# A static schedule for 32-head attention plus a gated feed-forward: free head order for ScalarE, units that change engine, a third score bank given by rules, and VectorE and GpSimd copies kept apart

## The chip, the cores and the metric

The kernel runs on one core of one Trainium2 chip. The metric is the device time of one execution in microseconds (us). Engines are named as in the profile: PE is TensorE, PEld its weight loads, ACT is ScalarE, DVE is VectorE, POOL is GpSimd, SP is SyncE.

## The reference, cut to what matters

```python
# x: 1 x 2048 x 512, 32 heads of 16; all bf16
g = sigmoid((x * gate_w).sum(-1, keepdims=True))
qkv = x @ wqkv
p = softmax(q @ k.T * 16 ** -0.5)          # 32 heads x 2048 x 2048 scores
a = (p @ v) @ wo
b = ((x @ w_gate) * (x @ w_up)) @ w_down   # inner width 1376
return g * a + (1 - g) * b
```

Attention has 134 million scores, and every one needs an exponential. That work sets the size of this kernel.

Of the kernel before, what the change touches and what calls it, by code (L numbers as in the profile page):

```python
# [10 lines left out]
ALU = mybir.AluOpType  # L11
# [160 lines left out]
FL = []  # L172

# [16 lines left out]
def _build(nc, A_x, A_wqkv, A_wo, W_gate, W_up, W_down, gate_w, out):  # L190
# [14 lines left out]
    NCELL = 46  # L205
    RA = 22
# [12 lines left out]
    with ExitStack() as stack:  # L219
# [18 lines left out]
        PT = sb("PT", [128, NCELL, 512], BF16)  # L238
# [4 lines left out]
        bsb = sb("bsb", [128, 2, 4, D], BF16)  # L243
# [66 lines left out]
        d_wv[0] = load("act", wv[:, :, 0:128], wcol(2 * D, 2 * D + 128), "dwv0", 0.5, 4.0)  # L310
# [18 lines left out]
        r_ = load("act", wv[:, :, 128:D], wcol(2 * D + 128, 3 * D), "dwv1", 0.55, 9.5)  # L329
        d_wv[1:] = [r_] * (NB - 1)  # L330
# [51 lines left out]
        cells = [_Cell() for _ in range(NCELL)]  # L382

        def cell_ap(c, n, dt=None):
            a = PT[:, c : c + n, :].rearrange("p a b -> p (a b)")
            return a if dt is None else a.bitcast(dt)
# [4 lines left out]

        def alloc(n, t, pair=False, keep=0):
            if pair:
                got = None
                for i in range(RA, NCELL, 2):
                    if is_free(i, t) and is_free(i + 1, t):
                        if got is None:
                            got = i
                        if keep == 0:
                            return got  # L400
                        keep -= 1
                return None
            for k in range(RA):
                i = (st["ring"] + k) % RA
                if i + n <= RA and all(is_free(x, t) for x in range(i, i + n)):
                    st["ring"] = i + n
                    return i
                if k > 3:
                    break
            return None  # L410
# [12 lines left out]
        pe = {"mode": "c"}  # L423

# [21 lines left out]
        class Fill:  # L446

            def __init__(self, name, packs, deps, evac, pos):
                self.name = name
                self.packs = packs  # L450
                self.deps = deps
                self.evac = evac
                self.pos = pos
                self.i = 0
                self.bank = None
                self.old = []
# [82 lines left out]
        def f_v(b, tg, pos):  # L539
            packs = []  # L540
            for t4 in range(4):
                t = 4 * tg + t4

                def mk(bk, t=t, t4=t4):
                    def fn(e):
                        r = None
                        for kt in range(KD):
                            for q in range(4):
                                r = e.matmul(
                                    bk.ap[32 * q : 32 * q + 32, t4 * 128 : (t4 + 1) * 128],  # L550
                                    xT[:, kt, t * 128 + 32 * q : t * 128 + 32 * q + 32],
                                    wv[:, kt, b * 128 : (b + 1) * 128],
# [9 lines left out]
                packs.append((mk, 0.36, "c"))  # L562

            def evac(bk, last):
                bk.need += 1
                ev_v[b, tg] = add(
# [3 lines left out]
                        VS[:, 4 * tg : 4 * tg + 4, 8 * b : 8 * b + 8, 0:Dh],  # L570
                        bk.ap.rearrange("p (t h d) -> p t h d", t=4, d=Dh),
# [5 lines left out]
                base = VS[:, 4 * tg, 8 * b, :]  # L577
                src = bass.AP(base.tensor, base.offset, [list(base.ap[0]), [(H + 2) * VW, 4], [1, 2 * VW]])
                for k in range(3):
                    dst = VD[:, k, 4 * tg : 4 * tg + 4, b, :, :].rearrange("p t a d -> p t (a d)")  # L580
                    ev_vd[b, tg, k + 1] = add(
                        "pool",
                        [ev_v[b, tg]],
# [5 lines left out]
            return Fill(f"v{b}{tg}", packs, lambda: [d_wv[b]] + xdep(tg), evac, pos)  # L589
# [43 lines left out]
        def f_u(c, f, pos):  # L633
# [24 lines left out]
            return Fill(f"u{c}.{f}", packs, lambda: [d_wu] + xdep(c), evac, pos)  # L658
# [32 lines left out]

        def f_d(c, tt, pos):
# [12 lines left out]
            def evac(bk, last):  # L705
# [4 lines left out]
                    [last, ogate["g"], bfree.get((c - 2, tt))],  # L710
                    lambda v: v.tensor_scalar(bsb[:, c % 2, tt, :], bk.ap, omg[:, t : t + 1], None, ALU.mult),  # L711
# [5 lines left out]
            def deps():  # L717
                if c >= 2 and (c - 2, tt) not in bfree:
                    return [None]
# [7 lines left out]
        def combine(t, bank_ap, last, cb=None, halves=None):  # L727
# [5 lines left out]
                    ost[:, t % 2, :], bank_ap, gval[:, t : t + 1], bsb[:, c % 2, tt, :], ALU.mult, ALU.add  # L733
# [5 lines left out]
            bfree[c, tt] = k  # L739
# [34 lines left out]
        AU = []  # L774
        for m in range(NM):
            for kt in range(T):
                for i in range(3):
                    AU.append((m, kt, (kt + 3 - i) % 4))
        DU = [[(m, 4 * i + j, j) for m in range(NM) for i in range(T // 4)] for j in range(4)]
        dnext = [0, 0, 0, 0]  # L780
        NA = len(AU)
        PER = NA // NM

# [15 lines left out]
        pv_left = [28 * 4] * NM  # L799
        first_pv = {}  # L800
# [4 lines left out]
        def add_tile(m, kt, j, k, cell, src):  # L805
            pvq[m, j].append((kt, k, cell, src))

        def run_scores(aus, dus, abanks, dbanks, t):
# [24 lines left out]
            k = pe_run(deps, fn, PACK, "r", t)  # L833
            for u, bk in us:
# [17 lines left out]
        def new_d(u, bk, sc):  # L852
# [5 lines left out]
            pr["u"].append(u)  # L858

# [9 lines left out]
            def cb(k):  # L869
                bk.readers.append(k)  # L870
                pr["p1"].append(k)
# [11 lines left out]

        def try_copy(eng, t):
            best = None
            for pr in pairs:
# [5 lines left out]
                if eng == "pool":  # L892
                    k = pr["k"][-1]
                else:
                    k = pr["k"][0]
                    if k == 3 and clock["pool"] < t + 0.5:
# [24 lines left out]
            else:  # L921
                fn = lambda g: g.tensor_scalar(cell_ap(c, n, I16), cell_ap(pr["cell"], n, I16), 32.0 * k, 1.0, ALU.add, ALU.mult)  # L922
                occ = 0.16 + 0.50 * n
# [6 lines left out]
        def tile_ok(m, tl, t):  # L930
# [4 lines left out]
            v = ev_v.get((b, kt // 4)) if k == 0 else ev_vd.get((b, kt // 4, k))  # L935
            return v is not None and v.end is not None and v.end + SEM <= t

        def pv_ready(t, partial=False):
# [6 lines left out]
            for j in range(4):  # L945
# [3 lines left out]
                elif not partial and first_pv.get((m, j), 0) < 28:  # L949
# [5 lines left out]
        def do_pv(got, t):  # L955
# [5 lines left out]
            for j, tl in got:  # L961
                kt, k, cell, src = tl
                pvq[m, j].remove(tl)
                deps += [src, ev_v[b, kt // 4] if k == 0 else ev_vd[b, kt // 4, k]]
# [6 lines left out]
                specs.append((j, kt, k, cell, s0, first_pv[m, j] == 28))  # L971
# [30 lines left out]
            for j, kt, k, cell, s0, s1 in specs:  # L1002
                cells[cell].readers.append(kk)
            if pv_left[m] == 0:
                pvst["m"] += 1
# [5 lines left out]
        def norm(m, last):  # L1011
# [29 lines left out]
            if p == 0 or (c == NCH - 1 and b == NB - 1):  # L1041
                dst, w_ = OT[:, g % NOT, :], otfree.get(g - NOT, [])
            else:
# [6 lines left out]
                prio=1,  # L1050
            )
# [21 lines left out]
        for ch in range(1, 4):  # L1073
            fills.append(f_k(0, ch, 0))
            fills.append(f_v(0, ch - 1, 0))
        fills.append(f_v(0, 3, 0))
        for b in range(1, NB):
            p0 = 96 * b
            sp = 84.0 if b > 1 else 56.0
            seq = [lambda pos: f_q(0, b, pos)]  # L1080
            lst = [("q", 0)] + [x for ch in range(4) for x in (("k", ch), ("v", ch))]
            for i, (kind, ch) in enumerate(lst):
                pos = p0 - sp + i * (sp - 14) / 8.0
                if kind == "q":
                    fills.append(f_q(0, b, pos))
                elif kind == "k":
                    fills.append(f_k(b, ch, pos + 0.0))
                else:
                    fills.append(f_v(b, ch, pos + 0.0))
        fills.append(f_gate(100.0))  # L1090
        f0, f1 = 100.0, 1470.0
        step = (f1 - f0) / NCH
        for c in range(NCH):
# [3 lines left out]
            seq += [("d", tt) for tt in range(4)]  # L1097
            w = [1.0] * 22 + [2.0] * 4
            acc = 0.0
            for (kind, i), ww in zip(seq, w):  # L1100
                pos = f0 + step * c + step * acc / sum(w)
                acc += ww
                fills.append({"u": f_u, "g": f_g, "d": f_d}[kind](c, i, pos))
        for c in range(NCH - 1):
            for tt in range(4):
                fills.append(f_wo(c, tt, PER * NQ * (c + 1) + 30.0 + 8.0 * tt))
            for b in range(NB):
                fills.append(f_q(c + 1, b, PER * NQ * (c + 1) - 30.0 + 96.0 * b - (40.0 if b else 0.0)))
        fills.sort(key=lambda f: f.pos)

        st = {"ua": 0, "slot": 0, "fill": None, "ring": 0}
# [17 lines left out]
        def start_fill(f, bk):  # L1129
            fills.remove(f)  # L1130
            f.bank = bk
            FL.append((f.name, f.pos, st["ua"], round(clock["pe"], 2), bk.name))
# [4 lines left out]
        def do_fill(t):  # L1137
# [5 lines left out]
            if f.i == len(f.packs):  # L1143
                f.bank.need -= 1
                f.evac(f.bank, k)
                st["fill"] = None
# [16 lines left out]
        LEAD = 2  # L1163

        def d_pick(js, t, lim):
            best = None
            mn = min([4 * dnext[j] + j for j in range(4)])
# [8 lines left out]

        def pe_step():
# [3 lines left out]
            more = ua < NA or any(dnext[j] < len(DU[j]) for j in range(4))  # L1181
            can = False
            tE = None
            if ua < NA and len(exps) < 2:
                n = min(3, NA - ua)
                fr = [s[i].free_at() for i in range(2)]
                if all(f is not None for f in fr) and all(kq_ready(AU[x], t) for x in range(ua, ua + min(2, n))):
# [4 lines left out]
            lag = ua / 3.0 - min(4 * dnext[j] + j for j in range(4))  # L1192
            if can and tE <= t and lag > 8 and not bank_free(X, t) and not bank_free(s[2], t):
                can = False
            if can and tE <= t:
                xf = X.free_at()
                wait_x = xf is None or xf + SEM > t
                if wait_x and t + PACK <= tL - 0.05:
                    if filler(t):
                        return True  # L1200
                n = min(3, NA - ua)
                fw = None
                if st["fill"] is None:
                    fw = fill_next(t)
                third = n == 3 and bank_free(s[2], t) and kq_ready(AU[ua + 2], t)
                if st["mq"] and st["slot"] == 0:
                    third = False
                if lag >= 3:
                    third = False
                elif third and fw is not None:  # L1210
# [258 lines left out]
```

## The kernel before: the parts that the change touches

Python code plays the five engines against a clock of its own while the program is built, and writes down for each engine the order in which it would start its work. The result is five fixed instruction lists with semaphores for data. No decision is left at run time. If the chip is slower somewhere than the builder believed, the order stays and the others wait.

The scores of four heads and 512 queries are computed against 128 keys at a time. One such 128 x 512 block of one head is a *unit*, 2048 in all. A quarter of them (`DU`) goes to DVE, three quarters (`AU`) to ACT. The exponentials lie in SBUF *cells* of 128 x 512 until PE has multiplied them with V (*PV* below) and the cell is free again.

```python
AU = []
for m in range(NM):                        # 32 groups of four heads x 512 queries
    for kt in range(T):                    # 16 key tiles
        for i in range(3):
            AU.append((m, kt, (kt + 3 - i) % 4))          # ACT: fixed order
DU = [[(m, 4 * i + j, j) for m in range(NM) for i in range(T // 4)] for j in range(4)]
```

ACT computes the exponentials of two or three units with one instruction (an *activation*). DVE uses a trick on the bits: adding a constant to the scaled score and storing it as int16 gives, read as bf16, a crude exponential. Its error is averaged out by adding four versions, shifted by 0, 32, 64 and 96, each multiplied with its own scaled V. So a DVE unit needs one drain of 128 x 512 from PSUM, three *copies* (SBUF to SBUF, int16, two units at a time, 128 x 1024; listed as PT<-PT), and four PV matmuls instead of one. The copies are shared with POOL:

```python
def try_copy(eng, t):                      # ... cut
    if eng == "pool":
        k = pr["k"][-1]
    else:
        k = pr["k"][0]
        if k == 3 and clock["pool"] < t + 0.5:
            continue
    # DVE: fn adds 32 * k, occ = 0.07 + 0.133 * n;   POOL: occ = 0.16 + 0.50 * n
```

The kernel divides PSUM into eight banks: two groups of three for scores (psS), one extra (psX), one for the PV sums (psO). A group's third bank can go to ACT, to DVE or to a *fill* (a projection or feed-forward matmul, placed at a position `pos` of the unit count). The choice before:

```python
third = n == 3 and bank_free(s[2], t) and kq_ready(AU[ua + 2], t)
# ... cut
if lag >= 3:                               # DVE is 3 units behind ACT's place: the bank is for DVE
    third = False
elif third and fw is not None:             # a fill is waiting: it takes the bank
    third = False
    start_fill(fw, s[2])
na = 3 if third else min(2, n)
aus = AU[ua : ua + na]                     # ACT first, DVE gets the heads that are left
js = [j for j in range(4) if j not in [u[2] for u in aus]]
```

The four heads of one score pass use different 32-row strips of PE, so a pass can hold at most one unit of each head, and it takes the same time with two units as with four (in the trace of before 388, 391 and 395 ns in the median for two, three and four units, from the first start to the last end).

The softmax here doesn't subtract the row's maximum and nothing guards it: scores larger than these inputs give would overflow.

## Time and profile before

| | before |
|---|---|
| median | 902.15 us (3 runs, 899.18 to 905.06) |
| profiled span | 907.3 us, mean granted clock 0.944 |

The profiled execution of before took 909.3 us. It is recorded as fast, but it is longer than every timed run here, and 1.6% above the fastest run of before in the result below (895.14 us).

First the head of the page of the kernel before: the busy time of each engine, its share and its instructions.

```profile
span 907.3 us, 22838 instructions
...
PE 765.7 (84%) x9718; PEld 217.2 (24%) x9718; DVE 768.0 (85%) x1229; ACT 736.5 (81%) x753; POOL 415.7 (46%) x406
```

Next the groups of the kernel before: count, then busy us and mean ns of one, then the engine's idle time just before them and what ended it.

```profile
L1302 ACT ACTIVATE PT<-psS 128x1024 bf16<-128x1024 f32 (+1 forms) x732 | 721.4, 1090 | 152.9 <-PE psS L823 136.5 <-PE psO L979 10.8 <-PE psS L990 1.9
L922 POOL TENSOR_SCALAR PT<-PT 128x1024 int16<-128x1024 int16 x315 | 356.7, 1143 | 401.7 <-DVE PT L877 248.5 <-PE psS L823 114.5 <-PE psO L979 30.5
L919 DVE TENSOR_SCALAR PT<-PT 128x1024 int16<-128x1024 int16 x453 | 319.1, 735 | 10.8 <-PE psO L979 2.4 <-PE psS L990 1.2
...
L877 DVE TENSOR_SCALAR PT<-psX 128x512 int16<-128x512 f32 x324 | 220.0, 679 | 56.9 <-PE psS L823 47.8 <-PE psO L979 7.6 <-PE psS L990 0.4
...
L877 DVE TENSOR_SCALAR PT<-psS 128x512 int16<-128x512 f32 x188 | 126.7, 677 | 5.0 <-PE psS L823 4.9
```

Three engines are between 81% and 85% busy, so none is the plain limit. ACT stands idle 153 us before its exponentials, nearly all of it for scores from PE. The copies (L919) take 735 ns on DVE, longer than a drain of half as many elements from PSUM (677 ns); that is odd for the cheaper operation.

The waits of the kernel before (total us, times, longest us) show the loop: PE waits for DVE and ACT to give banks back, and ACT waits for PE.

```profile
ACT PT L1302 <- PE psS L823: 136.5, 117, 11.6
PEld psX L823 <- DVE PT L877: 115.7, 172, 1.9
...
PEld psS L823 <- ACT PT L1302: 97.1, 203, 1.4
...
ACT PT L1302 <- PE psO L979: 10.8, 8, 2.4
```

And four stretches of the kernel before (from:to and length in us, then busy us of each engine, granted clock, DMA share, GB/s):

```profile
core 0: us, PE busy (x) PEld busy (x) DVE busy (x) ACT busy (x) POOL busy (x), PEclk, DMA share, GB/s
0.00:50.00 50.00, 41.72 (x653) 15.56 (x653) 29.64 (x56) 32.72 (x35) 19.51 (x36) 1.00 0.71 173
50.00:300.00 250.00, 209.76 (x3043) 65.17 (x3042) 208.84 (x337) 188.83 (x192) 113.36 (x125) 0.94 0.05 14
300.00:600.00 300.00, 259.89 (x2968) 66.89 (x2965) 269.36 (x429) 259.58 (x262) 141.29 (x124) 0.93 0.05 16
600.00:780.00 180.00, 152.01 (x1819) 40.53 (x1823) 162.85 (x257) 153.69 (x160) 87.85 (x77) 0.97 0.05 16
```

ACT is hungriest from 50 to 300 us: 189 of 250 us busy.

**Why the copies are slow.** Two rows of the timeline of the kernel before, one for DVE and one for POOL (start us, length us), show it. The first view is DVE's:

```profile
435.32 3.28 DVE L919 TENSOR_SCALAR PT<-PT 128x1024 int16<-128x1024 int16 x4
```

The second is POOL's:

```profile
432.57 5.42 POOL L922 TENSOR_SCALAR PT<-PT 128x1024 int16<-128x1024 int16 x5 [2.14 <-DVE PT L877]
```

Four DVE copies took 3.28 us while POOL was copying. Alone, a DVE copy lasts 408 ns and the next instruction starts 330 ns after it, so four would take about 1.4 us. Over the whole trace, 268 DVE copies start while a POOL instruction runs, and 267 of them end after it. (The exception began 10 ns after its POOL instruction and took 418 ns; there POOL ended 1.1 us after it.) Of the 250 that start with more than 0.2 us of the POOL instruction to go, the median ends 279 ns after POOL's end (8 in 10 between 277 and 281). This is no sharing of bandwidth: DVE waits until POOL has finished and then does its work. The Trainium skill says the same: "SBUF — State Buffer", section "SBUF: two separate sides", calls the port pair that VectorE's two-port modes share with GpSimd an exclusive lock, kept for the whole instruction. The trace agrees. DVE's work from PSUM (677 ns) is untouched by POOL (its drains take 675 ns apart from POOL and 678 beside it, in the median).

Below, *issue time* is the sum of the times from an instruction's start to the next one's start (at most its own length). The copies of before have 300 us of it on DVE; at 330 ns each they would have 149.

### The profile page before, as it was taken

To read this page: it belongs to the slowest core of one execution; us is meant where nothing else is said; L and a number is where in the kernel's file an instruction comes from. 1 tells how busy PE (TensorE), PEld (TensorE's weight loads), DVE (VectorE), ACT (ScalarE), POOL (GpSimd) and SP (SyncE) were. 2 spreads that over 40 slices of the span, in tenths; PEclk is the share of its full clock that TensorE was granted. 3 is DMA by queue.
4 is the path that set the end of the run, shared out by engine and by line. 5 is a ranking of instruction groups with operands and counts; after the bars stand their busy time and mean duration, and the time that the engine had idled before them with its cause. 6 is when DMAs were issued, how large, how long until landed. Compare 5 with 4: busy or idle time off the path is not lost. (4 is left out here: it accounts for less than half of the span.)

```text
span 907.3 us, 22838 instructions
## 1 busy us (share of the span) xinstructions
PE 765.7 (84%) x9718; PEld 217.2 (24%) x9718; DVE 768.0 (85%) x1229; ACT 736.5 (81%) x753; POOL 415.7 (46%) x406
## 2 busy tenths in 40 slices
PE   7998977887888888888989887888987887788995
PEld 2332223232222222222222122122222221222222
DVE  2988787987869999999898898799979998897784
ACT  3988865966759999899787795899968898688884
POOL 1566344444524554555444344255435564445441
PEclk9997799999999999999987799699999999999897
DMA  9500000000000000000000000000000010000000
GB/s 177 204 15 16 13 5 16 14 14 5 14 2 22 31 16 14 17 14 17 14 14 4 25 28 14 13 13 17 6 13 17 19 34 14 3 16 13 17 14 24
DMA packets 31020, 21.73 MB, mean 24 GB/s; under 512 B 18856, under 2 KB 25928, under 8 KB 30920
## 3 DMA queue, kind: packets, MB, share of 16 engines
q1 hardware_dynamic: 26936, 18.44, 7.0%
q10 hardware_dynamic: 3984, 1.84, 1.0%
q8 instruction: 77, 1.26, 0.6%
q14 instruction: 23, 0.19, 0.1%
HBM read 15.11 MB, written 2.35 MB: 19 GB/s over the span
## 5 line engine op out<-in xcount | busy, mean ns | idle before, releaser
L1302 ACT ACTIVATE PT<-psS 128x1024 bf16<-128x1024 f32 (+1 forms) x732 | 721.4, 1090 | 152.9 <-PE psS L823 136.5
L922 POOL TENSOR_SCALAR PT<-PT 128x1024 int16<-128x1024 int16 x315 | 356.7, 1143 | 401.7 <-DVE PT L877 248.5
L919 DVE TENSOR_SCALAR PT<-PT 128x1024 int16<-128x1024 int16 x453 | 319.1, 735 | 10.8 <-PE psO L979 2.4
L823 PE MATMUL psS<-QM,KE 32*128 32x512 bf16 x1724 | 297.5, 403 | 29.7 <-ACT PT L1302 17.5
L979 PE MATMUL psO<-PT,VS 128*18 128x512 bf16 x2048 | 274.8, 401 | 14.6 <-DVE oraw L1016 8.4
L877 DVE TENSOR_SCALAR PT<-psX 128x512 int16<-128x512 f32 x324 | 220.0, 679 | 56.9 <-PE psS L823 47.8
L979 PE MATMUL psO<-PT,VD 128*18 128x512 bf16 x1536 | 242.5, 401 | 16.0 <-DVE PT L919 9.5
L823 PE MATMUL psX<-QM,KE 32*128 32x512 bf16 x324 | 130.4, 402 | 55.8 <-DVE PT L877 34.7
L877 DVE TENSOR_SCALAR PT<-psS 128x512 int16<-128x512 f32 x188 | 126.7, 677 | 5.0 <-PE psS L823 4.9
L823 PEld LDWEIGHTS psS<-QM,KE 32*128 32x128 bf16 x1724 | 70.3, 91 | 193.8 <-ACT PT L1302 97.1
L979 PEld LDWEIGHTS psO<-PT,VS 128*18 128x18 bf16 x2048 | 62.7, 89 | 84.4 <-issue 43.0
L823 PEld LDWEIGHTS psX<-QM,KE 32*128 32x128 bf16 x324 | 29.6, 91 | 191.0 <-DVE PT L877 115.7
L979 PEld LDWEIGHTS psO<-PT,VD 128*18 128x18 bf16 x1536 | 54.8, 89 | 69.6 <-issue 30.5
L471 PE MATMUL psS<-xT,wu 128*32 128x512 bf16 x596 | 51.4, 407 | 0.2 <-DVE hT L679 0.2
L471 PE MATMUL psS<-wd,hT 128*32 128x512 bf16 (+1 forms) x616 | 51.2, 404 | 0.0
L471 PE MATMUL psS<-xT,wg 128*32 128x512 bf16 x596 | 48.9, 395 | 0.0
L1048 POOL TENSOR_TENSOR OX<-oraw,rb 128x512 bf16<-128x512 f32 x15 | 19.3, 1287 | 26.4 <-DMA rb<-rscr 25.5
L652 DVE CAST usb<-psS 128x512 bf16<-128x512 f32 (+1 forms) x38 | 25.7, 675 | 6.2 <-PE psS L471 6.1
L1048 POOL TENSOR_TENSOR OT<-oraw,rb 128x512 bf16<-128x512 f32 x16 | 21.3, 1330 | 17.3 <-DMA rb<-rscr 17.3
L584 POOL TENSOR_SCALAR VD<-VS 128x144 bf16<-128x144 bf16 x48 | 15.9, 331 | 27.3 <-DVE VS L569 24.7
L679 DVE TENSOR_TENSOR hT<-psS,usb 128x512 bf16<-128x512 f32 (+1 forms) x38 | 25.6, 673 | 2.2 <-PE psS L471 2.2
L1016 DVE COPY oraw<-psO 128x512 f32<-128x512 f32 x31 | 20.9, 676 | 0.6 <-PE psO L979 0.6
(82 smaller groups left out, 322.2 us busy)
## 6 DMA issues: line engine op xcount, KB each, us to landing
rb<-rscr SPq DMA_DIRECT2D x31, 256.0 KB
out_dram<-ost SPq DMA_DIRECT2D x16, 128.0 KB, 1.7
wu<-in_B_w_up_dram SPq DMA_DIRECT2D x1, 1376.0 KB, 6.7
wg<-in_B_w_gate_dram SPq DMA_DIRECT2D x1, 1376.0 KB, 10.7
wd<-in_B_w_down_dram SPq DMA_DIRECT2D x1, 1280.0 KB, 12.4
OT<-OX SPq DMA_DIRECT2D x60, 16.0 KB, 1.8
wo<-in_A_wo_dram SPq DMA_DIRECT2D x1, 512.0 KB, 9.5
den<-oraw SPq DMA_DIRECT2D x31, 8.0 KB
```

The costliest lines, as they stand in the source:

```text
L471: return e.matmul(out_ap[32 * q : 32 * q + w, :], lhs[:, 32 * q : 32 * q + w], rhs, start=s0, stop=s1, tile_position=(0, 32 * q), skip_gro ...
L584: lambda g, k=k, dst=dst, src=src: g.tensor_scalar(dst, src, WK[k + 1], 1.0, ALU.mult, ALU.mult),
L652: lambda v: v.tensor_copy(usb[0:w, n % 2, :], bk.ap[0:w, :]),
L679: lambda v: v.tensor_tensor(hT[0:w, f, :], bk.ap[0:w, :], usb[0:w, n % 2, :], ALU.mult),
L823: r = e.matmul(bk.ap, KE[32 * j : 32 * j + 32, b, kt * 128 : (kt + 1) * 128], QM[32 * j : 32 * j + 32, p, b, :], start=True, stop=True, ti ...
L877: lambda v: v.tensor_scalar(cell_ap(pr["cell"] + i, 1, mybir.dt.int16), bk.ap, CB, 0.0, ALU.add, ALU.max),
L919: fn = lambda v: v.tensor_single_scalar(cell_ap(c, n, I16), cell_ap(pr["cell"], n, I16), 32.0 * k, ALU.add)
L922: fn = lambda g: g.tensor_scalar(cell_ap(c, n, I16), cell_ap(pr["cell"], n, I16), 32.0 * k, 1.0, ALU.add, ALU.mult)
L979: r = e.matmul(psO[32 * j : 32 * j + VW, :], pv_stationary(m, kt, j, k), cell_ap(cell, 1), start=s0, stop=s1, tile_position=(0, 32 * j), s ...
L1016: "dve", [last, o_mult.get(m - NO)], lambda v: v.tensor_copy(oraw[:, s, :], psO[:]), 0.61, prio=1
L1048: lambda e: e.tensor_tensor(dst, oraw[:, s, :], rb[:, s, :], ALU.mult),
L1302: lambda a: a.activation(cell_ap(c, n), src, ACT.Exp, scale=LN2 / 128.0),
```

## The change

The intent is to keep ACT busy. The change is one version step with several parts; lines for bookkeeping are cut.

(1) ACT takes units of any head, the oldest ready first; DVE's heads are chosen first. If DVE lags by more than 3 units, its next unit becomes ACT's (a *conversion*).

```diff
-        AU = []
+        AQ = [[] for _ in range(4)]
         for m in range(NM):
             for kt in range(T):
                 for i in range(3):
-                    AU.append((m, kt, (kt + 3 - i) % 4))
+                    j = (kt + 3 - i) % 4
+                    AQ[j].append((64 * m + 4 * kt + i, (m, kt, j)))
+        def a_pick(js, n, t):
+            c = sorted((AQ[j][0][0], j) for j in js if AQ[j] and kq_ready(AQ[j][0][1], t))
+            return [j for _, j in c[:n]]
+        def convert():
+            j = min(range(4), key=lambda j: 4 * dnext[j] + j)
+            u = DU[j][dnext[j]]
+            dnext[j] += 1
+            AQ[j].insert(0, (64 * u[0] + 4 * u[1] + 3, u))
...
+                if dleft and lag > LC:          # LC = 3
+                    convert()
```

(2) The third bank goes by rules that differ for the two groups; DVE may also use the other group's third bank.

```diff
-                if lag >= 3:
-                    third = False
-                elif third and fw is not None:
-                    third = False
+                if own:
+                    use3 = "a"
+                    if late > (FA1 if b else FA0):        # -99 and 12
+                        use3 = "f"
+                    elif lag >= (LA1 if b else LA0):      # 0 and 2
+                        use3 = "d"
+                if use3 != "f" and bank_free(so[2], t) and lag >= LA1 and not (st["mq"] and so[2] is DB) and st["slot"] == 0:
+                    db.append(so[2])
```

(3) In the builder, a DVE copy and any POOL instruction exclude each other, and POOL only takes the third copy, and only while DVE has other work.

```diff
+            if eng == "pool" and t < lock["dve"]:
+                clock[eng] = lock["dve"]
+                return True
...
-                c = try_copy(eng, t)
+                if eng == "pool" or lock["pool"] <= t:
+                    c = try_copy(eng, t)
...
+            if eng == "pool" and dve_busy(t) < 0.45:
+                return None
...
                 if eng == "pool":
                     k = pr["k"][-1]
+                    if k != 3:
+                        continue
```

(4) Fills are spread: K and Q of later heads just ahead of need, V for two groups at once (half as many matmuls, twice as wide), feed-forward from unit 205 instead of 100, and away from psX.

(5) The cells that hold exponentials grow from 46 to 58: an intermediate buffer is dropped (its contents go to the K and Q weights once those are no longer needed), and four cells lie in the V weights after their last use. A search for the smallest gap that fits replaces a ring, in which the search went on from the last place.

```diff
-    NCELL = 46
-    RA = 22
+    NMAIN = 54
+    NCELL = NMAIN + 4
+    RA = 26
```

Three further rules of the scheduler changed with these: DVE may run 5 units ahead instead of 2 (`LEAD`), a pass for DVE alone is made when it lags by more than 8 (`LDO`), and a pass is held back while psX or the third bank is not free and ACT still has work.

## The prediction

> **What bounds it now.** No single engine. The page's busy shares are PE 84%, DVE 85%, ACT 81%, POOL 46%; in the stretch view 300 to 400 us has DVE 95, ACT 94, PE 86 of 100 us, but 100 to 300 us has ACT at only 72 to 73. Three nearly full engines run in a closed loop: in the waits view PE's score loads wait 116 us for DVE to drain psX and 97 us for ACT, ACT waits 137 us for scores.
>
> DVE is full partly for a bad reason. The SBUF-to-SBUF scaled copies (PT<-PT, 453) average 735 ns in the group table. Sorted by overlap with a POOL instruction, 84 without overlap have a median of 408 ns and 330 ns start to start; those with overlap start about 780 ns apart. POOL's copies grow from 1046 to 1209 ns. The Trainium skill, "GPSIMD Engine Reference", Specifications, says that SBUF interfaces are shared with VectorE, contended by DVE instructions in a 2-port mode; this trace agrees. PSUM-source DVE work (677 ns, 598 start to start) is the same with or without POOL.
>
> **What the change does** (counts from the instruction order, prices from the trace):
> 1. It keeps DVE copies and POOL work apart in the static schedule. 453 DVE + 315 POOL copies become 498 + 243. DVE copies cost about 300 us of issue time now; 498 at 330 ns cost 164: about -135 us of DVE, if the chip keeps the planned separation; only order and data waits enforce it, so I count on two thirds to all.
> 2. It converts 19 DVE score units to ACT: DVE -19 x 0.6 = -11 us; 57 fewer PV matmuls (-3 us of PE).
> 3. ACT: 658 activations of 1024 + 73 of 1536 become 512 + 177. At 904 and 1331 ns start to start: 692 us before, 698 after. No relief; ACT must be fed better (153 us idle now).
> 4. PE: runs of score matmuls number 658 before, 663 after, so the tile switches (320 ns start to start across one, 215 to 220 within a mode) stay. V projection has half the matmuls at double width (-7 us). About 715 us of natural PE time becomes 695; reduced clock (mean 0.944) adds some 50.
> 5. Cells 46 to 58, freer choice of third bank, fill matmuls on psX from 788 to 244, FFN fill starting later: less waiting, above all in 50 to 300 us.
>
> **Critical path.** Afterwards DVE needs 620 to 650 us, ACT 700, PE 745 including clock. Start (first exponential at 17 us) and tail (16 us after the last PV) stay. The floor is about 775; a closed loop with one engine at 90% gives about 825. DVE's gain is only partly worth time: of 145 us freed I expect some 80 to show, as PE and ACT become the limit.
>
> **Predicted: 822 us, range 785 to 860** (8 in 10). Faster by over 2%: 0.95; within 2%: 0.04; slower: 0.01.
>
> **What would show it.** DVE copies averaging 410 to 520 ns; POOL copies 1050 to 1100; DVE busy about 640 us, under 80%; ACT busy 735 to 750 us, share near 90%; PE share 88 to 92%; ACT's wait for scores under 90 us; PE's wait for psX clearly below 116 us; ACT above 82% in 100 to 300 us. Granted clock 0.93 to 0.97.
>
> **What would make it wrong.** If the run drifts from the plan, DVE and POOL copies meet again, DVE stays near 750 us and only fills and banks gain (870). If PE's switches or reduced clock bind harder than I assume, it ends near 855. If feeding works nearly perfectly, 790.

## The result

| | before | after |
|---|---|---|
| median of fast runs | 900.66 us (4 runs, 895.14 to 905.06) | 802.14 us (4 runs, 797.04 to 805.80) |
| ratio to before | 1 | 0.8905 (95%: 0.883 to 0.898) |
| profiled span | 907.3 us | 797.8 us |
| granted clock | 0.944 | 0.973 |

A ratio here is the mean time of one kernel's fast runs over that of the other's fast runs of the same rounds, so it is not quite the ratio of the medians quoted beside it.

The head of the page of the kernel after:

```profile
span 797.8 us, 21597 instructions
...
PE 711.6 (89%) x9149; PEld 206.4 (26%) x9149; DVE 711.2 (89%) x1255; ACT 734.4 (92%) x710; POOL 331.5 (42%) x334
```

Its groups that answer to those shown of before. The exponentials are in two lines now, because the extra cells lie in the buffer wv:

```profile
L1446 ACT ACTIVATE PT<-psS 128x1024 bf16<-128x1024 f32 (+1 forms) x572 | 614.5, 1190 | 44.5 <-PE psS L861 28.9 <-PE psO L1035 13.6
L975 DVE TENSOR_SCALAR PT<-PT 128x1024 int16<-128x1024 int16 (+1 forms) x498 | 276.1, 594 | 7.9 <-PE psO L1035 2.3 <-PE psS L1046 1.1
...
L978 POOL TENSOR_SCALAR PT<-PT 128x1024 int16<-128x1024 int16 x243 | 273.0, 1125 | 355.5 <-DVE PT L919 190.5 <-PE psO L1035 75.6 <-PE psS L861 71.5
...
L919 DVE TENSOR_SCALAR PT<-psX 128x512 int16<-128x512 f32 x316 | 214.6, 679 | 28.1 <-PE psS L861 24.8 <-PE psO L1035 1.8
L1446 ACT ACTIVATE wv<-psS 128x1024 bf16<-128x1024 f32 (+1 forms) x117 | 134.1, 1160 | 6.7 <-PE psS L861 6.2
...
L919 DVE TENSOR_SCALAR PT<-psS 128x512 int16<-128x512 f32 x177 | 118.8, 679 | 11.2 <-PE psS L861 9.0 <-PE psO L1035 1.8
```

Its waits:

```profile
PEld psX L861 <- DVE PT L919: 71.9, 132, 2.1
...
PEld psS L861 <- ACT PT L1446: 68.4, 154, 1.0
...
ACT PT L1446 <- PE psS L861: 28.9, 48, 5.6
...
ACT PT L1446 <- PE psO L1035: 13.6, 6, 4.5
...
ACT wv L1446 <- PE psS L861: 6.2, 9, 1.8
```

The same stretches:

```profile
0.00:50.00 50.00, 43.83 (x623) 16.46 (x627) 32.87 (x62) 36.32 (x39) 19.96 (x44) 1.00 0.68 173
50.00:300.00 250.00, 221.85 (x2986) 67.42 (x2982) 229.74 (x398) 229.21 (x217) 106.32 (x110) 0.98 0.05 16
300.00:600.00 300.00, 276.53 (x3477) 75.61 (x3481) 281.56 (x505) 291.18 (x284) 131.77 (x115) 1.00 0.06 17
600.00:780.00 180.00, 161.78 (x1959) 43.87 (x1955) 162.65 (x285) 165.25 (x157) 73.46 (x65) 0.93 0.06 18
```

**Where the time went.** ACT does nearly the same work in both (1536 units before, 1555 after), so its line can be cut up without remainder. From the trace: the time to the first exponential, the issue time of the exponentials, the time between them, and the time from the last one's end to the end.

| us | to first | issue | between (idle) | after last | sum |
|---|---|---|---|---|---|
| before | 17.2 | 721.4 | 144.6 | 24.1 | 907.3 |
| after | 14.9 | 719.3 | 45.7 | 18.0 | 797.9 |

Of 109 us between the two profiled spans, 98.9 are idle time of ACT that is gone, 8.4 lie at the two ends, and 2.1 in ACT's work. (The medians differ by 98.5 us only, since the profiled run of before was a long one.) ACT's wait for scores fell from 137 to 35 us (28.9 + 6.2), and in 300 to 600 us it is 97% busy (291 of 300). ACT is now the fullest engine. That it is the limit is argued, not shown: no run changed ACT's work alone.

**A rival: the granted clock.** It was 0.944 in the profiled run of before and 0.973 in that of after. A straight line through the 22 fast runs of before that came with the experiments (clock 0.945 to 0.973, 903.93 to 889.98 us) falls by 3.7 us for each 0.01 of clock; one through the ten runs of after (0.954 to 0.977) falls by 4.3. At 0.965 the two lines give 895.4 and 801.9 us, an estimate of 10.4% instead of 11%. On one chip and at one clock, 0.971, single runs took 893.7 us before and 798.11 after. So the clock explains little of the change. The lines do not show whether a low clock lengthens a run or comes with what lengthens it.

DVE gained less than planned. Its copies still average 594 ns. A quarter of them (0.25, against 0.49 before) last over 600 ns, because 167 still start inside a POOL instruction. The lock's cost, the copies' issue time above 330 ns each, fell from 151 to 96 us.

### The profile page after: what moved, and what is told of

The parts are those of the page before. It is cut to its first block, busy times and chain, and to the rows that moved or that the text cites. A ratio compares the mean times of both kernels' runs of the same rounds, so it can differ in the third digit from the quotient of the medians.

```text
span 797.8 us, 21597 instructions
## 1 busy us (share of the span) xinstructions
PE 711.6 (89%) x9149; PEld 206.4 (26%) x9149; DVE 711.2 (89%) x1255; ACT 734.4 (92%) x710; POOL 331.5 (42%) x334
## 5 line engine op out<-in xcount | busy, mean ns | idle before, releaser
L1446 ACT ACTIVATE PT<-psS 128x1024 bf16<-128x1024 f32 (+1 forms) x572 | 614.5, 1190 | 44.5 <-PE psS L861 28.9
L978 POOL TENSOR_SCALAR PT<-PT 128x1024 int16<-128x1024 int16 x243 | 273.0, 1125 | 355.5 <-DVE PT L919 190.5
L861 PE MATMUL psS<-QM,KE 32*128 32x512 bf16 x1732 | 273.4, 391 | 17.1 <-ACT PT L1446 9.5
L975 DVE TENSOR_SCALAR PT<-PT 128x1024 int16<-128x1024 int16 (+1 forms) x498 | 276.1, 594 | 7.9 <-PE psO L1035 2.3
L1035 PE MATMUL psO<-PT,VS 128*18 128x512 bf16 x1791 | 241.0, 390 | 6.1 <-DVE PT L975 2.7
L1035 PE MATMUL psO<-PT,VD 128*18 128x512 bf16 x1479 | 227.6, 387 | 9.2 <-DVE PT L975 4.8
L861 PE MATMUL psX<-QM,KE 32*128 32x512 bf16 x316 | 122.5, 388 | 24.6 <-DVE PT L919 10.9
L1446 ACT ACTIVATE wv<-psS 128x1024 bf16<-128x1024 f32 (+1 forms) x117 | 134.1, 1160 | 6.7 <-PE psS L861 6.2
L919 DVE TENSOR_SCALAR PT<-psS 128x512 int16<-128x512 f32 x177 | 118.8, 679 | 11.2 <-PE psS L861 9.0
L1035 PE MATMUL psO<-wv,VS 128*18 128x512 bf16 x257 | 71.9, 393 | 1.3 <-POOL PT L978 1.0
```

What stands on the lines that cost most here:

```text
L861: r = e.matmul(bk.ap, KE[32 * j : 32 * j + 32, b, kt * 128 : (kt + 1) * 128], QM[32 * j : 32 * j + 32, p, b, :], start=True, stop=True, ti ...
L919: lambda v: v.tensor_scalar(cell_ap(pr["cell"] + i, 1, mybir.dt.int16), bk.ap, CB, 0.0, ALU.add, ALU.max),
L975: fn = lambda v: v.tensor_single_scalar(cell_ap(c, n, I16), cell_ap(pr["cell"], n, I16), 32.0 * k, ALU.add)
L978: fn = lambda g: g.tensor_scalar(cell_ap(c, n, I16), cell_ap(pr["cell"], n, I16), 32.0 * k, 1.0, ALU.add, ALU.mult)
L1035: r = e.matmul(psO[32 * j : 32 * j + VW, :], pv_stationary(m, kt, j, k), cell_ap(cell, 1), start=s0, stop=s1, tile_position=(0, 32 * j), s ...
L1446: lambda a: a.activation(cell_ap(c, n), src, ACT.Exp, scale=LN2 / 128.0),
```

## The experiments

Two theories were set against each other. The *feeding theory*: the gain comes from the picking rules (heads, banks, fills), which keep ACT supplied. The *port theory*: it comes from keeping DVE copies and POOL apart, which frees DVE. Each run is compared with the kernel before on the same chip. "Idle" and "issue" of ACT are cut as in the table above.

| run | median us | ratio to before, 95% | ACT issue / idle us | DVE copy, mean ns | DVE issue us |
|---|---|---|---|---|---|
| before | 900.66 | 1 | 721.4 / 144.6 | 735 | 768 |
| after | 802.14 | 0.8905 (0.883 to 0.898) | 719.3 / 45.7 | 594 | 711 |
| e1 before, tiny POOL copies | 831.41 | 0.9285 (0.923 to 0.934) | 708.1 / 85.4 | 457 | 657 |
| e2 after, no separation | 816.75 | 0.9126 (0.907 to 0.919) | 726.2 / 53.5 | 727 | 729 |
| e3 before, with separation | 926.84 | 1.0351 (1.029 to 1.042) | 716.8 / 164.3 | 608 | 745 |
| e4 after, enforced | 794.01 | 0.8871 (0.883 to 0.892) | 716.9 / 42.1 | 421 | 634 |
| e5 after, fixed heads | 845.59 | 0.9426 (0.938 to 0.947) | 714.2 / 88.0 | 581 | 726 |
| e6 after, no conversion | 816.99 | 0.9094 (0.904 to 0.915) | 714.9 / 54.3 | 592 | 730 |
| e7 after, old third bank | 832.31 | 0.9283 (0.924 to 0.933) | 756.9 / 39.3 | 665 | 652 |
| e8 after, old fills | 814.78 | 0.9081 (0.903 to 0.913) | 726.6 / 59.5 | 634 | 721 |
| e9 after again (control) | 800.25 | 0.8900 (0.886 to 0.894) | 719.6 / 44.7 | 599 | 713 |
| e10 enforced, tuned | 778.04 | 0.8657 (0.862 to 0.870) | 714.4 / 27.0 | 422 | 634 |
| e11 before, separation enforced | 889.86 | 0.9900 (0.985 to 0.995) | 712.7 / 132.3 | 422 | 656 |
| e12 after, old cells | 807.86 | 0.8988 (0.896 to 0.902) | 717.2 / 54.7 | 589 | 714 |

All results are correct except that of e1. e1 to e4 ran on one chip, e5 to e8 on another, e9 to e12 on a third, each set with its own runs of before; kernels of different sets are compared by their ratios to before.

### e1: what the lock costs in the kernel before

```diff
-  fn = lambda g: g.tensor_scalar(cell_ap(c, n, I16), cell_ap(pr["cell"], n, I16), 32.0 * k, ...)
+  fn = lambda g: g.tensor_scalar(cell_ap(c, n, I16)[:, 0:8], cell_ap(pr["cell"], n, I16)[:, 0:8], 32.0 * k, ...)
```

The copy cells are set to zero once at the start; apart from that, the instruction order is that of before.

> The kernel before in its exact instruction order, with each POOL copy cut to 8 of its 1024 columns (results wrong on purpose; the cells are zeroed once at the start, about 3 us of VectorE). It prices the contention between POOL and VectorE copies in the kernel before, together with POOL's time. Feeding theory (most of the 100 us came from keeping ScalarE fed by the new picking rules): VectorE copies fall from 735 to about 420 ns and VectorE busy by about 130 us, yet the time falls only to 850 to 880 us. Port theory (most of the 100 us came from separating POOL and VectorE copies): 830 us or less.

Measured: 831.41 us, ratio 0.9285. It falls between the two expectations, nearer to the port theory, so the feeding theory's 850 to 880 was a miss. In the loop of before, the lock and POOL's time together are worth up to 64 us (895.43 of before less 831.41). They cannot be parted here: the tiny copies free DVE, and they also deliver their results about 0.9 us earlier (POOL's copies average 271 ns instead of 1143).

### e2: the kernel after without the separation

```diff
-            if eng == "pool" and t < lock["dve"]:
-                clock[eng] = lock["dve"]
-                return True
-                if eng == "pool" or lock["pool"] <= t:
...
-            if eng == "pool" and dve_busy(t) < 0.45:
-                return None
-                    if k != 3:
-                        continue
```

> The kernel after with the rules of the kernel before for who takes a scaled copy and when (no mutual exclusion, POOL takes any of the three copies). All else as after. Feeding theory: VectorE copies back to about 700 ns, time 815 to 835 us. Port theory: 860 us or more.

Measured: 816.75 us. The group of DVE's copies in e2:

```profile
L971 DVE TENSOR_SCALAR PT<-PT 128x1024 int16<-128x1024 int16 x429 | 299.7, 727 | 9.1 <-POOL PT L974 1.5 <-PE psO L1031 1.1
```

The copies are as slow as before (the last detail of the rule, how long DVE leaves the third copy to POOL, and POOL's assumed cost went back as well), and yet the time is 8.7% below before, of the 11% of the whole change. ACT's idle time is 54 us against 46. In the changed kernel the separation is worth 0.9126/0.8905, or 2.5%. This is what the feeding theory said.

### e3: the kernel before with only the separation

The reverse of e2's edit, made in the kernel before.

> The kernel before with only the separation of POOL and VectorE copies added (mutual exclusion and the new rules for who takes a copy). Feeding theory: 870 to 900 us, ACT's wait for scores still over 100 us. Port theory: 850 us or less, VectorE copies about 600 ns as in the kernel after.

Measured: 926.84 us, 3.5% *slower* than before, which neither theory expected. The copies did get faster (608 ns) and DVE's issue time fell by 23 us. The waits of e3 show what it cost:

```profile
ACT PT L1317 <- PE psS L824: 135.3, 83, 15.8
...
POOL PT L937 <- PE psO L994: 113.3, 45, 14.3
...
ACT PT L1317 <- PE psO L994: 34.7, 21, 5.1
```

ACT waits for scores as long as before (135 us), and in addition 35 us (11 before) for PV to free cells; POOL waits 113 us for PV, against 31. The same rules that help the new kernel by 2.5% hurt the old one. But all four runs of e3 had a lower granted clock (0.922 to 0.930) than the fast runs of before in the same call (0.959 to 0.973). The line of before, drawn on below the clocks that it was measured at, would give 910 us at 0.925. By this estimate about half of the 3.5% goes with the clock, and why the clock was lower is not shown. Run e11 returns to this.

### e4: the separation enforced

```diff
                     c = try_copy(eng, t)
                     if c is not None:
+                        o_ = lasts.get("pool" if eng == "dve" else "dvec")
+                        if o_ is not None:
+                            c.deps = c.deps + [o_]      # a semaphore wait
                         run_task(c, t)
+                        lasts["dvec" if eng == "dve" else "pool"] = c
...
+            if eng == "pool" and lasts.get("dvec") is not None:
+                best.deps = best.deps + [lasts["dvec"]]
             run_task(best, t)
```

PE, DVE, ACT and POOL run exactly the instructions of the kernel after in the same order (the two traces agree one by one); only waits are added.

> The kernel after in its exact instruction order, with the planned separation enforced by semaphores: each VectorE copy waits for the last POOL instruction planned before it, and each POOL instruction for the last VectorE copy planned before it. If the contention that is left (copies 594 ns instead of 412) costs time, 790 us or less with copies at about 420 ns; if ScalarE is the limit and VectorE has slack, 795 to 810 us, the same within 1%; if the new waits stall VectorE as long as the contention did, VectorE idle rises by as much as its busy time falls (about 80 us).

Measured: 794.01 us. The page's head and the copies of e4:

```profile
PE 716.5 (90%) x9149; PEld 208.7 (26%) x9149; DVE 634.0 (80%) x1255; ACT 732.0 (92%) x710; POOL 310.3 (39%) x334
...
L976 DVE TENSOR_SCALAR PT<-PT 128x1024 int16<-128x1024 int16 (+1 forms) x498 | 188.8, 421 | 66.6 <-POOL PT L979 29.8 <-POOL OT L1108 10.0 <-POOL VD L608 5.3
```

No DVE copy starts inside a POOL instruction any more; the mean is 421 ns, and DVE's busy time falls by 77 us, from 711.2 to 634.0. The time falls by 0.4% in the ratios (0.8871 against 0.8905), and the intervals overlap; at the clocks of e4 (0.961 to 0.968) the line of after gives about 1%, across chips. The freed time became idle time of DVE: span less busy is 159 us, against 87. So while ACT is 92% busy, 77 us less of DVE buy almost nothing. The prediction of this run missed both of its numbers (790 or less, 795 or more) by landing between them; the third clause, idle for busy, is what the trace shows.

### e5: ACT's heads in the old fixed order, no conversion

```diff
-        LC = 3
+        LC = 10**9
...
                 nmax = 3 if use3 == "a" else 2
+                ajs = a_pick(range(4), nmax, t)          # the oldest units, whatever their head
...
-                    d = d_pick([j for j in range(4) if j not in djs], t, lim)
+                    d = d_pick([j for j in range(4) if j not in djs + ajs], t, lim)
...
-                if use3 == "d" and s[2] not in dbs:
-                    nmax = 3
-                ajs = a_pick([j for j in range(4) if j not in djs], nmax, t)
```

The edit takes out one thing more: after, a third bank that was meant for DVE and that DVE cannot use goes to ACT (`nmax = 3`).

> The kernel after with ScalarE's units taken in the one fixed order of before (heads chosen first for ScalarE, VectorE gets what is left) and with no conversion of VectorE units. All else as after. Theory of heads (free head order is the largest part of the gain): 840 us or more, ACT waiting over 80 us for scores. Rival theory of banks and fills (third bank and even fills are the largest part): within 2.5% of after, 800 to 820 us.

Measured: 845.59 us, the largest loss of any part: 0.9426/0.8905, or 5.9%. The page of e5 shows how:

```profile
PE 773.9 (92%) x9206; PEld 211.7 (25%) x9206; DVE 725.9 (86%) x1290; ACT 729.4 (87%) x789; POOL 342.9 (41%) x345
```

And its main ACT group, from the groups by shape:

```profile
L1444 ACT ACTIVATE PT<-psS 128x1024 bf16<-128x1024 f32 x663 | 628.6, 1092 | 85.9 <-PE psO L1035 60.8 <-PE psS L861 23.7
```

PE is 62 us busier than in the kernel after (773.9 against 711.6). The trace has 859 score passes instead of 689, and the instruction order 775 runs of score matmuls between other work instead of 663. Each run costs two switches between the 32-row and the 32-column tiling of PE: start to start takes 315 ns across a switch in the median, and 205 to 225 ns within one tiling. The Trainium skill, "TensorEngine Tiling (Array Packing)", section "Key Properties", says that a change of tiling mode drains the engine, which agrees; the price of about 0.1 us is from this trace. An estimate from these numbers: 170 more passes at 0.22 us are 37 us, and 224 more switches at 0.1 us are 22, together about the 62 us. Of the 859 passes, 91 hold no unit for ACT (none do so in the kernel after): by the rule `LDO`, a DVE that finds no fitting head and lags gets passes of its own. And no activation takes three units (177 after). With PE at 92%, PV comes late, and ACT waits for cells (psO 60.8 us). The expected sign, ACT waiting over 80 us *for scores*, was wrong: that wait is 26 us (23.7 here, 2.7 in the group that writes wv); the shortage shows at the other end of the loop.

### e6: free heads, but no conversion

```diff
-        LC = 3
+        LC = 10**9
```

> The kernel after without the conversion of lagging VectorE units to ScalarE (19 units); free head order kept. 512 score drains on VectorE instead of 493. If taking over units matters: 812 us or more. If it only tidies the balance: 800 to 812 us.

Measured: 816.99 us, a loss of 2.1%, for moving 19 of 2048 units. Nineteen drains are 11 us of DVE, so the balance of work is not the point. The activations tell: the kernel after has 512 activations of two units and 177 of three; e6 has 752 and 10. The groups of three in the kernel after, by shape:

```profile
L1446 ACT ACTIVATE PT<-psS 128x1536 bf16<-128x1536 f32 x154 | 230.1, 1494 | 19.5 <-PE psO L1035 10.6 <-PE psS L861 8.3
...
L1446 ACT ACTIVATE wv<-psS 128x1536 bf16<-128x1536 f32 x23 | 34.2, 1489 | 0.4 <-PE psS L861 0.2
```

And those of e6:

```profile
L1446 ACT ACTIVATE PT<-psS 128x1536 bf16<-128x1536 f32 x9 | 13.5, 1504 | 0.5 <-PE psS L861 0.5
...
L1446 ACT ACTIVATE wv<-psS 128x1536 bf16<-128x1536 f32 x1 | 1.5, 1458 | 0.0
```

By the new rule a lagging DVE claims the third bank; without conversion the lag is not brought down, and ACT hardly ever gets a group of three. Score passes rise from 689 to 767 and PE busy from 712 to 741 us. The conversions keep the lag under the threshold and so keep passes full. Between e5 and e6 (neither converts; heads fixed, without the bank's fallback, or free) lie 0.9426/0.9094, or 3.7%.

### e7: the old rule for the third bank

```diff
-                    if late > (FA1 if b else FA0):
-                        use3 = "f"
-                    elif lag >= (LA1 if b else LA0):
-                        use3 = "d"
+                    if lag >= 3:
+                        use3 = "d"
+                    elif fw is not None:
+                        use3 = "f"
...
-                if use3 != "f" and bank_free(so[2], t) and lag >= LA1 ...:
-                    db.append(so[2])
```

Fills outside a score pass also go back to psX alone.

> The kernel after with the rule of before for the third score bank: VectorE gets it only when it lags by 3 or more, a waiting fill takes it else, never the other group's third bank, and fills outside a score run use only psX. The conversion then triggers about 112 times, so ScalarE does more units (about 1650 instead of 1555, about 40 us more of work). Theory of banks: 840 us or more. Theory of heads: 805 to 830 us.

Measured: 832.31 us, a loss of 4.2%, between the two expectations. ACT's idle time is even lower (39 us), but it has 38 us more of work. The group of DVE's drains from psX in e7:

```profile
L919 DVE TENSOR_SCALAR PT<-psX 128x512 int16<-128x512 f32 x359 | 245.6, 684 | 121.9 <-PE psS L861 120.1 <-PE psO L1035 0.2
```

DVE waits 120 us for scores (25 in the kernel after) and does 400 drains instead of 493, since 112 units were converted to ACT. So the bank rules are what feeds *DVE* its share; without them the conversion saves ACT from idling by giving it DVE's work. The granted clock was 0.944 to 0.946 in all runs of e7, lower than in any run of after; the line of after, drawn on to 0.945, gives 810.5 us, so by this estimate about a third of the loss goes with the clock.

### e8: the old fill positions

```diff
-        GP = 200.0
-        F0 = 205.0
-        F1 = 1490.0
+        GP = 100.0
+        F0 = 100.0
+        F1 = 1470.0
-                fills.append(f_q(c + 1, b, PER * NQ * c + 96.0 * (b + 1) + 30.0))
+                fills.append(f_q(c + 1, b, PER * NQ * (c + 1) - 30.0 + 96.0 * b - (40.0 if b else 0.0)))
```

The positions of the first K, Q and V fills and of the output fills go back too.

> The kernel after with the fill positions of before (projections and feed-forward fills from score unit 100 on, output fills and queries as before); the wide V projection is kept. If the even fill order matters: 815 us or more, ACT below 85% busy in 50 to 300 us. If it does not: 798 to 810 us.

Measured: 814.78 us, a loss of 2.0%, ACT idle 60 us against 46. It just missed the "815 or more" of one branch, and ACT was 91% busy (227 of 250 us) in 50 to 300 us, not below 85%. So the fill order matters by about 2%, but it is not what cured the hungry stretch.

### e9 to e12: control, an enforced and tuned version, two last parts

e9 is the kernel after, unchanged.

> The kernel after, unchanged, as the control of this call on the same chip: 797 to 808 us, ratio to before 0.885 to 0.896.

Measured: 800.25 us, ratio 0.8900.

e10 is e4 with two numbers of the scheduler moved.

```diff
-        LEAD = 5
-        FA0 = 12
+        LEAD = 8
+        FA0 = 20
```

> The enforced separation again, with two numbers of the scheduler moved (VectorE may run 8 instead of 5 units ahead; a fill must be 20 instead of 12 late before it takes the first group's third bank). If enforcing is a true gain: below the control of this call by 0.7 to 2% with intervals that do not overlap, VectorE copies at about 420 ns. If the 1% seen before was the chip's: within 0.5% of the control.

Measured: 778.04 us, ratio 0.8657. That is 2.7% below the control of the same chip, with intervals far apart, more than the 0.7 to 2% expected, and the fastest kernel. Its page:

```profile
span 774.6 us, 21680 instructions
...
PE 711.8 (92%) x9158; PEld 204.8 (26%) x9158; DVE 633.8 (82%) x1259; ACT 729.5 (94%) x723; POOL 313.0 (40%) x336
```

ACT's idle time is down to 27 us. How much of the 2.7% comes from enforcing and how much from the two numbers stays open: the two numbers alone did not run. e4 suggests that enforcing alone gives about 1% at most.

e11 is e3 with the enforcing edit of e4.

> The kernel before with the separation rules (the run that came out 3.5% slower than before), now enforced by semaphores in the same instruction order, so that the contention that was left (copies 608 ns) is gone. If it was slower because of contention left: 890 us or less. If the rules hold copies back and so keep cells and banks busy (POOL's wait for PV was 113 us against 31): 905 to 930 us, although VectorE copies fall to about 420 ns and VectorE busy by about 80 us.

Measured: 889.86 us, which meets the first branch: removing the contention that was left turns 1.0351 into 0.9900, a gain of 4.4%. So the contention that was left costs e3 more than it lost against before. Why is not shown: e3's copies paid 107 us for the lock, less than the 151 us of before. (e11 also ran at a higher clock than e3, 0.927 to 0.954; by the line of before that is about 0.6 of the 4.4%.) But even with clean copies, the old picking rules reach only 1% below before. The ACT groups of e11:

```profile
L1318 ACT ACTIVATE PT<-psS 128x1024 bf16<-128x1024 f32 (+1 forms) x738 | 712.7, 1114 | 138.5 <-PE psS L825 107.7 <-PE psO L995 28.8 <-PE psS L1006 1.0
```

DVE is only 74% busy, and ACT still stands idle 138 us. e1 and e11 have the same DVE issue time (657 and 656 us) and differ by nearly 7% in time, so DVE's amount of work is not what sets the time of this kernel.

e12 is the kernel after with the old number of cells.

```diff
-    NMAIN = 54
-    RA = 26
+    NMAIN = 46
+    RA = 22
-            cells[i].need = NB * NCH
+            cells[i].need = 10**6          # the four cells in wv are never freed for use
```

> The kernel after with 46 cells as before (22 for ScalarE, 24 for copies) instead of 58. If cells matter in themselves: 815 us or more, with ACT waiting longer for PV (psO). If the 46 were enough for the new rules: 800 to 810 us.

Measured: 807.86 us, 1.0% above the control, intervals apart. The cells matter a little; the 46 were nearly enough.

### What the parts are worth

Taken out one at a time, the parts cost 5.9% (head order with conversion; 2.1% the conversion alone), 4.2% (bank rules), 2.5% (separation), 2.0% (fills) and 1.0% (cells). Their sum, 15.6%, is more than the whole change, since putting all of it back costs 1/0.8905 or 12.3%. So the parts overlap: each covers some of the same shortage when another is missing. The three rules named at the end of "The change" have no price of their own.

## Why the prediction was right or wrong

- **The time.** 822 us predicted, 785 to 860; measured 802.14 us. Faster by over 2% (0.95) was right.
- **What bounds the kernel before.** "Three nearly full engines run in a closed loop" stands. The loop's weak member was ACT's supply: 98.9 of the 109 us between the profiled spans were idle time of ACT.
- **Point 1, separation: mis-sized.** The prediction had "about -135 us of DVE" for the copies and counted on "two thirds to all". Measured: the copies' issue time fell from 300 to 260 us, with 45 more of them, so the lock's cost fell by 55 us, a little over a third. In the prediction's own term that is -40 us instead of -90 to -135. Copies averaged 594 ns, not 410 to 520, POOL's copies 1125 ns instead of 1050 to 1100, and DVE was busy 711 us, not 640. The doubt that the prediction named, that only order and data waits enforce the plan, came true for 167 copies.
- **The step from DVE to time: wrong.** "Of 145 us freed I expect some 80 to show." DVE's issue time fell by 57 us, and the time fell by 98. e2 keeps the copies slow (727 ns) and is still 8.7% below before; e4 frees 77 us more and gains 0.4%. The prediction's own branch for copies that meet again, with only fills and banks gaining, said 870 us; e2 comes close to that case and took 816.75. So that the predicted total came out near the truth is partly luck: the gain from feeding, which the prediction named in point 5 but gave no number, outweighed what DVE fell short of.
- **Point 2, conversion: the count was right, its worth was not.** The prediction priced 19 units at 11 us of DVE. e6 shows 2.1% of the time, since the conversions keep the lag low and give ACT 177 groups of three instead of 10.
- **Point 3, ACT's work unchanged: right.** Issue time 721.4 and 719.3 us; busy 734 us, just under the 735 to 750 forecast; share 92% against "near 90%".
- **Point 4, PE: right on the whole.** Share 89% (forecast 88 to 92%), but 711.6 us busy where 745 were expected. The clock was 0.973, just above the forecast range of 0.93 to 0.97. The tile switches stayed (658 and 663 runs), and e5 and e6 show what they cost where they do not.
- **Point 5, less waiting: right, and too modest.** ACT's wait for scores is 35 us ("under 90"), PE's wait for psX 72 us ("clearly below 116"), and ACT is busy 184 of 200 us from 100 to 300 us ("above 82%").
- **The limit.** "PE and ACT become the limit": the two are the fullest in the best run, e10, with ACT at 94% and PE at 92%. e4 shows that DVE is not the limit; that ACT is was not tested.

## What to carry to other kernels

Find the engine whose work cannot be reduced, cut its line into work and idle time, and judge a change by the idle time that it removes. A large saving on a neighbour that has slack (77 us here) may buy next to nothing (0.4 to 1%), and the same rule may help one schedule and hurt another (2.5% here, -3.5% there, about half of it with a lower clock). Where a fixed order only hopes that two engines stay out of each other's way, an explicit wait costs little and makes the plan true.

## What the Trainium skill lacked or had wrong

- "GPSIMD Engine Reference", section 1 "Specifications", names the contention with VectorE without a size; "SBUF — State Buffer", section "SBUF: two separate sides", gives the lock. Neither says how long a VectorE copy takes after a GpSimd instruction ends (the one such figure in the second is for the opposite order). Here it ends 279 ns after it (8 in 10 between 277 and 281 ns), and 267 of the 268 copies of before that started inside a GpSimd instruction, and 165 of the 167 of after, outlasted it.
- "TensorEngine Tiling (Array Packing)", section "Key Properties", says that a change of tiling mode drains the engine, without a price. Here start to start is 315 ns across a switch in the median and 205 to 225 ns within a tiling, so about 0.1 us per switch, some 1300 times in either kernel.
- No page weighs an added wait that keeps VectorE and GpSimd apart. Here the waits took VectorE's busy time from 711.2 to 634.0 us, with the time unchanged within the intervals (ratios to before of 0.8871 and 0.8905).
